# Split attention heads: the product with v in two passes, the sums of rows on VectorE

## The chip, the cores and the metric

The kernel runs on one core of a Trainium2 chip. The metric is the device time of one execution in microseconds. Three executions of the kernel before took 1229.11, 1231.16 and 1234.45 us; the median is 1231.16 us.

The engines are called as in the profile: PE is TensorE's matmul and PEld its loads of weights, DVE is VectorE, ACT is ScalarE, POOL is GpSimd, SP is the queue that issues most DMAs.

## The reference

Attention with a decay that is summed along the sequence, over 64 heads (8 batches of 8 heads, 576 positions, 64 columns a head), and then an MLP with a squared ReLU over all 4608 tokens:

```
scores = q @ k.T / 8
cum = cumsum(log(clip(f, 1e-4, 1)))
scores = where(causal, -1e9, scores + cum[i] - cum[j])
attn = exp(scores - max(scores)); attn /= sum(attn) + 1e-9
x = heads of attn @ v side by side          # 4608 x 512
out = relu(x @ w_in)**2 @ w_out             # 512 -> 2048 -> 512
```

Everything is float32.

## The kernel before, in words

**Two kinds of heads.** TensorE takes float32 whole, which is slow, or in the rounded type fp32r, which is fast. The first 14 heads (`NWHOLE`) work on whole numbers. The other 50 are *split*: a number is a rounded high part and a rounded rest, and a product of two numbers is made of passes over the parts. The MLP is split throughout (x into xh and xl, the weights and g likewise). This text is about the split heads.

**Units and slots.** A head has six units, in this order (keys in blocks of 128, the last of 64):

| unit | key block | queries | columns |
|---|---|---|---|
| 0 | 0 | 256 to 575 | 320 |
| 1 | 2 | 256 to 575 | 320 |
| 2 | 3 | 384 to 575 | 192 |
| 3 | 4 | 512 to 575 | 64 |
| 4 | 1 | 128 to 575 | 448 |
| 5 | 0 | 0 to 255 | 256 |

Scores stand transposed: keys on the partitions, queries along the columns. One slot (the loop over `n`, lines 684 to 710) traces one unit's scores and whatever is due beside them. In the slot of a unit stand, in this order: its scores and exp (`score`, lines 356 to 391), the products with v of the unit two slots earlier (`LAG` is 2; `av_part`, lines 413 to 448), a step of a finished pair of heads (`finish`), events of the first half, `fill(n, 0.5)`, events of the second half, `fill(n, 1.0)`. Each of PE, ACT, DVE, POOL and (after the opening) SP keeps the order of tracing.

**A split unit.** Two matmuls make the scores (lines 371 and 374). ACT takes exp into p (line 384); where the block lies on the diagonal (units 1 to 5), POOL masks its first square (line 386). `split_p` (lines 393 to 403) then makes ph, rounded by ACT (line 399), and the rest pl on DVE (line 400). It is put off: `split_last` traces it when the next MLP half is placed, or at the latest at the next slot's start. `av_split` (lines 405 to 411) makes three passes into the bank: high part of v with pl, rest of v with ph, high part of v with ph. The high part of v has a 65th column of ones, so that row 64 of the bank is the sum of p over the keys, the softmax's denominator.

**The bank of the products.** While the MLP runs there is one bank, 0. The queries 256 to 575 (the right part) gather in it over units 0 to 4; ACT then copies the result (line 446) and the row of denominators (line 448) out. Queries 0 to 255 (the left part) follow in the same bank, from unit 5 and a piece of unit 4, in unit 1's slot of the next head, and are copied out likewise.

**A pair of heads** is divided together (lines 450 to 474), in four parts at slots that `DIVIDE` gives, counted from the slot after the pair's last unit, less one: the denominators go to a compact tile by DMA (part 0), DVE adds 1e-9 and takes reciprocals and a DMA stores them to memory (part 1), two DMAs spread each row over 64 partitions of `den` (part 2), and POOL multiplies (part 3, line 473). `den` has two buffers, `wmag` (the weights' magnitudes, line 181) has one.

**v.** `load_v` fetches v of a head; `split_v` (lines 305 to 314) rounds it on DVE (line 311) and takes the rest on POOL (line 312), in the second half of unit 4's slot of the head before.

**q and k** are loaded into `qkraw` and rounded by `prep` (lines 285 to 303): r2 and kl0 on DVE, l2 and r1 on ACT, the rests on POOL.

**The MLP** is placed between the units in halves: `mlp1` (lines 497 to 515: twelve matmuls of 256 columns into bank 4, then r on ACT, g = r * r on DVE, gh = r * r rounded on ACT, gl = g - gh on DVE), and `mlp2` (lines 517 to 533: six matmuls of 512 columns) of the step before. `fill` (lines 604 to 622) counts how many halves are to be done at n + part: they are spread evenly from `ready[b-1]` to `ready[b]`, where `ready` is the slot of part 3 of the batch's last pair plus 2 (line 602). A batch lets 2, sometimes 3, chunks of 256 tokens run, of 32 halves each; the 48 slots of a batch thus hold 64 halves, once 96. `split_x` (lines 479 to 495) rounds x for a chunk on DVE.

## Time and profile before

| | |
|---|---|
| median of three executions | 1231.16 us |
| the profiled execution's own time | 1234.24 us |
| its span, first to last instruction | 1232.5 us |
| mean granted clock of TensorE | 0.990 |
| PE busy | 1181.0 us (96%) |
| PEld busy | 1048.0 us (85%) |
| DVE busy | 775.6 us (63%) |
| ACT busy | 700.0 us (57%) |
| POOL busy | 409.0 us (33%) |

Matmuls are pipelined: a matmul's busy time overlaps the next one's, so what one costs is read from the distance between starts or from the chain of waits, not from its mean duration. On DVE and ACT, too, the next instruction may start a little before the last has ended. In the views a row is a start, a duration, the engine, the line, the operation, out<-in and the shape; in square brackets stands the idle time of the engine before it and what ended it.

The first 14 heads and the conversion of the weights take about the first 200 us; the split heads follow to about 1080 us; the rest is MLP alone.

### The profile page before, as it was taken

What the parts mean: (1) busy time and instruction counts of PE and PEld (TensorE: products, weight loads), DVE (VectorE), ACT (ScalarE), POOL (GpSimd) and SP (SyncE); (2) the same over time, 40 slices, a digit from 0 to 9 for tenths busy, and PEclk for the clock granted to TensorE, in tenths of its full rate; (3) what the DMA queues carried; (4) which work ended last, traced back from release to release, by engine and by line L of the source; (5) the groups of instructions that cost most, each with busy time, mean ns of one, the idle gap of its engine ahead of it and who ended that gap; (6) DMA issues with size and microseconds to landing.
All of it is one profiled execution on the core that took longest, in us unless ns stands there. A gap on an engine that the chain in (4) does not pass through costs nothing.

```text
span 1232.5 us, 23332 instructions
## 1 busy us (share of the span) xinstructions
PE 1181.0 (96%) x7652; PEld 1048.0 (85%) x7652; DVE 775.6 (63%) x2045; ACT 700.0 (57%) x1720; POOL 409.0 (33%) x669
## 2 busy tenths in 40 slices
PE   4886999999999999999999999999999999999998
PEld 2554887888998899999999989998998899999997
DVE  7667875677676767666655676667676667533322
ACT  2563655566666566665655666666666666633232
POOL 4563544433333333332222233334333433200000
PEclk9997999999999999999999999999999999999999
DMA  7887531111121212121102121212121212000000
GB/s 178 184 169 173 160 102 43 36 49 41 42 58 41 59 37 49 33 56 36 49 16 58 27 58 42 58 36 49 32 58 42 58 41 58 12 27 1 18 18 18
DMA packets 114978, 71.62 MB, mean 58 GB/s; under 512 B 96909, under 2 KB 96909, under 8 KB 114857
## 3 DMA queue, kind: packets, MB, share of 16 engines
q1 hardware_dynamic: 113736, 66.00, 22.0%
q0 software_dynamic: 1120, 4.13, 1.8%
q8 instruction: 61, 1.00, 0.3%
q14 instruction: 61, 0.49, 0.1%
HBM read 59.90 MB, written 9.87 MB: 57 GB/s over the span
## 4 chain that ended last, share of the span: by engine, by line
PE 85%; DMA 5%; DVE 3%; ACT 3%; issue 2%; POOL 1%; SPq 1%; DVEq 0%; POOLq 0%; ACTq 0%
PE bank L503 32%; PE bank L526 30%; PE bank L326 3%; PE bank L409 3%; PE bank L374 3%; PE bank L411 3%; PE bank L410 3%; PE bank L371 3%; DMA rl<-tcol 2%; PE bank L432 2%; PE bank L365 2%; DVE bank L332 1%; DMA w<-in_w_in 1%; ACT den L448 0%; ACT r L511 0%
## 5 line engine op out<-in xcount | busy, mean ns | idle before, releaser
L526 PE MATMUL bank<-w,gh 128*128 128x512 f32 x1152 | 414.1, 400 | 0.0
L503 PE MATMUL bank<-xh,w 128*128 128x256 f32 x2304 | 331.9, 287 | 2.8 <-DVE tcol L332 2.2
L503 PEld LDWEIGHTS bank<-xh,w 128*128 128x128 f32 x2304 | 302.8, 190 | 11.4 <-DVE tcol L332 2.4
L400 DVE TENSOR_TENSOR pl<-p,ph 128x320 fp32r<-128x320 f32 (+4 forms) x300 | 182.1, 607 | 202.7 <-ACT ph L399 196.1
L526 PEld LDWEIGHTS bank<-w,gh 128*128 128x128 f32 x1152 | 217.5, 189 | 38.4
L526 PE MATMUL bank<-w,gl 128*128 128x512 f32 x576 | 226.8, 394 | 0.1
L511 ACT ACTIVATE r<-bank 128x256 f32<-128x256 f32 x288 | 110.3, 383 | 199.2 <-PE bank L503 181.0
L512 DVE TENSOR_TENSOR g<-r 128x256 f32<-128x256 f32 x288 | 128.6, 447 | 145.2 <-ACT r L511 144.6
L386 POOL TENSOR_SCALAR_AFFINE_SELECT p<-p 128x128 f32<-128x128 f32 (+1 forms) x250 | 80.8, 323 | 417.3 <-ACT p L384 276.1
L399 ACT CAST ph<-p 128x320 fp32r<-128x320 f32 (+4 forms) x300 | 124.4, 415 | 151.1 <-POOL p L386 149.3
L503 PE MATMUL bank<-xl,w 128*128 128x256 f32 x1152 | 185.0, 283 | 0.0
L503 PEld LDWEIGHTS bank<-xl,w 128*128 128x128 f32 x1152 | 159.0, 191 | 0.0
L384 ACT ACTIVATE p<-bank 128x320 f32<-128x320 f32 (+4 forms) x300 | 115.9, 386 | 64.9 <-PE bank L374 53.4
L514 DVE TENSOR_TENSOR gl<-g,gh 128x256 fp32r<-128x256 f32 x288 | 127.2, 442 | 35.0 <-PE bank L526 0.5
L332 DVE CUSTOM_DVE_ANT_0 bank<-bank,mz 128x256 f32<-128x256 f32 (+4 forms) x320 | 133.1, 432 | 24.7 <-PE bank L326 20.6
L326 PE MATMUL bank<-rk 66*128 66x320 f32 (+9 forms) x384 | 109.2, 315 | 22.9 <-DMA rk<-qkraw 10.6
L513 ACT ACTIVATE gh<-r 128x256 fp32r<-128x256 f32 x288 | 120.4, 418 | 9.2
L526 PEld LDWEIGHTS bank<-w,gl 128*128 128x128 f32 x576 | 109.2, 190 | 14.1 <-DVE gl L514 0.9
L409 PE MATMUL bank<-pl,vh 128*65 128x320 f32 (+4 forms) x350 | 96.8, 277 | 2.3 <-ACT den L448 2.3
L214 POOL TENSOR_TENSOR w<-osb,w 128x128 fp32r<-128x128 f32 x128 | 72.9, 597 | 77.9 <-ACT w L210 57.5
L326 PEld LDWEIGHTS bank<-rk 66*128 66x128 f32 (+3 forms) x384 | 68.3, 185 | 32.4 <-DVE tcol L332 12.6
L410 PE MATMUL bank<-ph,v 128*64 128x320 f32 (+4 forms) x350 | 94.6, 270 | 0.0
(83 smaller groups left out, 1558.3 us busy)
## 6 DMA issues: line engine op xcount, KB each, us to landing
qkraw<-in_qk SPq DMA_DIRECT2D x50, 288.0 KB
v<-in_v SPq DMA_DIRECT2D x62, 160.0 KB
out<-osb SPq DMA_DIRECT2D x36, 256.0 KB
den<-rdr SPq DMA_DIRECT2D x62, 144.0 KB
w<-in_w_in SPq DMA_DIRECT2D x16, 512.0 KB
w<-in_w_out SPq DMA_DIRECT2D x16, 512.0 KB
rk<-in_qk POOLq DMA_DIRECT2D x14, 288.0 KB, 5.4
rl<-in_qk SPq DMA_DIRECT2D x14, 288.0 KB
```

The source lines that it names most:

```text
L326: nc.tensor.matmul(ps[:m, :n], st["r2"][:rows, q0:q0 + m], st["kl0"][:rows, k0:k0 + n], start=True, stop=True,)
L332: nc.vector.tensor_tensor_reduce(out=ps[:m, :n], in0=ps[:m, :n], in1=mz[:m, mo:mo + n], op0=ALU.add, op1=ALU.min, scale=-1.0, scalar=init, ...
L384: nc.scalar.activation(out=p[:kn, :n], in_=ps[:kn, :n], func=AF.Exp, scale=SCALE)
L399: nc.scalar.copy(out=ph[:, :n], in_=p[:, :n])
L400: nc.vector.tensor_tensor(out=pl[:, :n], in0=p[:, :n], in1=ph[:, :n].bitcast(F32), op=ALU.subtract,)
L409: nc.tensor.matmul(acc[:D + 1, o], vh, pl[:, i], start=first, stop=False)
L410: nc.tensor.matmul(acc[:D, o], vl, ph[:, i], start=False, stop=False)
L503: nc.tensor.matmul(ph[:, :T], w[:, s, cc], x[:, cc, :], start=(cc == 0 and k == 0), stop=(cc == NCC - 1 and k == 2),)
L512: nc.vector.tensor_tensor(out=g, in0=r, in1=r, op=ALU.mult)
L513: nc.scalar.activation(out=gh, in_=r, func=AF.Square)
L514: nc.vector.tensor_tensor(out=gl, in0=g, in1=gh.bitcast(F32), op=ALU.subtract)
L526: nc.tensor.matmul(po, g[:, ts], w[:, s], start=(fc == 0 and k == 0), stop=(fc == NF - 1 and k == 2),)
```

## The change

**Products with v.** The tile of a head's v now holds the high part in columns 0 to 63 and the rest in 64 to 127. One pass of all 128 columns with ph gives the high product in the bank's rows 0 to 63 and the rest's product in rows 64 to 127; a second pass of 64 columns adds the high part with pl. The first product of a bank starts with the wide pass, so that it clears all 128 rows. Instead of the row of denominators, ACT copies rows 64 to 127 out, to a tile xl; when the pair is divided, DVE adds xl to x.

**Sums of rows.** As there is no column of ones, the denominators come from p itself, by `sum_p` right behind `split_p`. Units 0 and 5 write exp straight into a tile `total` (128 x 576, in the buffer of `wmag`), DVE adds the other units' p to it, and reduces it over 32 keys at a time with a transposing reduction: after unit 4 for the right part (320 columns), after unit 5 for the left (256). A DMA (`store_sums`) writes four partial sums for each query to memory; `finish` fetches those of a pair, adds them with 1e-9 in a fifth place, takes reciprocals and stores them in two DMAs.

**Buffers and order.** `den` has one buffer in turn, which xl and the spread denominators share. `DIVIDE` for batches after the first is 2, 4, 5, 6 and no longer 2, 4, 6, 7. As `ready` follows from its last entry, the split of a batch's first x and the start of its MLP move one slot earlier too. v of the first eight heads lies in buffers of weights that are converted later, and v of heads 8 to 13 is fetched three slots later. `qkraw` is one fixed tile; whole heads put their row of denominators in its row 64.

**MLP and q.** g is squared on ACT, from r, and no longer multiplied on DVE. The rest of q is taken against r2 (DVE's rounding) and no longer against r1 (ACT's).

```diff
     def split_v(h):
         if NWHOLE <= h < NH:
             st = state[h]
             vr = st["vr"][:, :, :D]
-            vh = st["vh"] = vhs[h % 2]
-            st["vl"] = wk.tile([P, NJ, D], F32R, name="v", bufs=3)
-            nc.vector.tensor_copy(out=vh[:, :, :D], in_=vr)
+            v = st["vhl"] = vhls[h % 2]
+            nc.vector.tensor_copy(out=v[:, :, :D], in_=vr)
             nc.gpsimd.tensor_tensor(
-                out=st["vl"], in0=vr, in1=vh[:, :, :D].bitcast(F32), op=ALU.subtract,
+                out=v[:, :, D:], in0=vr, in1=v[:, :, :D].bitcast(F32), op=ALU.subtract,
             )
...
         st["p"][u] = ph, pl
+        sum_p(h, u, p)
+
+    def sum_p(h, u, p):
+        st = state[h]
+        _, q0, q1 = UNITS[u]
+        total = totals[0]
+        def add(p, q0, q1):
+            nc.vector.tensor_tensor(
+                out=total[:, q0:q1], in0=total[:, q0:q1], in1=p, op=ALU.add,
+            )
+        def columns(o, q0, q1):
+            n = (q1 - q0) // 32
+            nc.vector.tensor_reduce(
+                out=st["sums"][:, o:o + n], in_=total[:, q0:q1].rearrange("p (i c) -> p c i", c=n),
+                axis=mybir.AxisListType.X, op=ALU.add, apply_transpose=True,
+            )
+        if 0 < u < NU - 1:
+            add(p[:, max(QA - q0, 0):q1 - q0], max(q0, QA), q1)
+            if q0 < QA:
+                st["rest"] = p[:, :QA - q0], q0, QA
+        if u == NU - 2:
+            st["sums"] = wk.tile([P, NC], F32, name="sums")
+            columns(0, QA, S)
+        if u == NU - 1:
+            add(*st.pop("rest"))
+            columns(NH1, 0, QA)
+
+    def store_sums(h):
+        st, i = state[h], h % 2
+        st["sdr"] = state[h - 1]["sdr"] if i else dr.tile([4, D, NC], F32, name="sdr")
+        nc.sync.dma_start(out=st["sdr"][:, i * 32:(i + 1) * 32], in_=st["sums"])
 
     def av_split(st, acc, u, o, i, first, last):
         j = UNITS[u][0]
         ph, pl = st["p"][u]
-        vh, vl = st["vh"][:, j, :D + 1], st["vl"][:, j, :]
-        nc.tensor.matmul(acc[:D + 1, o], vh, pl[:, i], start=first, stop=False)
-        nc.tensor.matmul(acc[:D, o], vl, ph[:, i], start=False, stop=False)
-        nc.tensor.matmul(acc[:D + 1, o], vh, ph[:, i], start=False, stop=last)
+        vhl = st["vhl"][:, j]
+        high = acc[:, o], vhl, ph[:, i]
+        low = acc[:D, o], vhl[:, :D], pl[:, i]
+        for k, args in enumerate((high, low) if first else (low, high)):
+            nc.tensor.matmul(*args, start=first and k == 0, stop=last and k == 1)
...
             nc.scalar.copy(out=x, in_=acc[:D, :n])
-            m = D if replicated(h) else 1
-            nc.scalar.copy(out=st["den"][o:o + m, base:base + n], in_=acc[D:D + m, :n])
+            if h >= NWHOLE:
+                nc.scalar.copy(out=st["xl"][o:o + D, base:base + n], in_=acc[D:, :n])
...
+            else:
+                nc.vector.tensor_tensor(out=x, in0=x, in1=st["xl"], op=ALU.add)
+                r = wk.tile([P, NC], F32, name="sums")[:D]
+                nc.vector.tensor_reduce(
+                    out=r, in_=parts.rearrange("p g c -> p c g"), axis=mybir.AxisListType.X, op=ALU.add,
+                )
+                nc.vector.reciprocal(out=r, in_=r)
+                for o, q0, q1 in (0, QA, S), (NH1, 0, QA):
+                    nc.sync.dma_start(
+                        out=st["rdr"][:, q0:q1].rearrange("h (p c) -> h p c", p=32),
+                        in_=r[:, o:o + (q1 - q0) // 32],
+                    )
         if part == 2:
+            den = st["den"] = wk.tile([P, S], F32, name="den", bufs=1)
...
-        nc.vector.tensor_tensor(out=g, in0=r, in1=r, op=ALU.mult)
+        nc.scalar.activation(out=g, in_=r, func=AF.Square)
         nc.scalar.activation(out=gh, in_=r, func=AF.Square)
...
-    DIVIDE = (2, 6, 9, 13), (2, 4, 6, 7)
+    DIVIDE = (2, 6, 9, 13), (2, 4, 5, 6)
...
+            at((h + 1) * NU, 1, store_sums, h)
```

88 lines of the change are left out of this document (54 added, 34 removed).

## The prediction

> **What bounds the kernel now.** I read the page first, then the busy times by stretches, the chain of waits through two heads, and the order of time of the same stretch on all engines.
>
> The page: span, busy time of TensorE, and the granted clock in 40 slices.
>
> ```profile
> span 1232.5 us, 23332 instructions
> PE 1181.0 (96%) x7652; PEld 1048.0 (85%) x7652; DVE 775.6 (63%) x2045; ACT 700.0 (57%) x1720; POOL 409.0 (33%) x669
> PEclk9997999999999999999999999999999999999999
> ```
>
> Busy time by stretches (span, then PE, PEld, DVE, ACT, POOL): one among the split heads.
>
> ```profile
> 300.00:350.00 50.00, 50.00 (x344) 45.69 (x343) 34.95 (x95) 33.28 (x84) 17.28 (x28) 1.00 0.19 46
> ```
>
> TensorE is never idle in it, at clock 1.00. DVE and ACT are two thirds busy among the heads. Time taken off TensorE is therefore gained, if the engines that empty the banks can follow. The chain of waits through the same heads (start, us on the chain) prices each piece of TensorE's work:
>
> ```profile
> 859.77 0.21 PE bank L371
> ...
> 860.27 0.09 PE bank L410
> ...
> 862.21 0.06 PE bank L410
> ...
> 862.33 1.51 PE bank L503 x12
> 863.84 1.39 PE bank L526 x6
> 865.24 0.15 PE bank L371
> ...
> 865.68 0.15 PE bank L410
> ...
> 865.98 1.43 PE bank L503 x12
> ...
> 867.83 0.12 PE bank L410
> ...
> 868.13 0.06 PE bank L410
> ...
> 870.00 0.28 PE bank L409
> ```
>
> A pass costs 0.21, 0.15, 0.12, 0.09, 0.06 and 0.06 us at 448, 320, 256, 192, 128 and 64 columns, an mlp1 1.43, an mlp2 1.39. The last row is a wait of 0.13 (0.28 against 0.15): unit 0's product finds bank 0 not yet emptied.
>
> **What TensorE saves.** Line 410 goes: per split head three passes of 320 columns, one each of 256, 192, 128, 64: 0.45 + 0.12 + 0.09 + 0.06 + 0.06 = 0.78 us. The kept high pass now has 128 weight columns, not 65. Twelve mlp1 matmuls behind a 64-column pass take 1.51, behind a 320-column pass 1.43: a load of 128 weight columns needs 0.08 more than the 0.03 that 64 columns move (half of the 0.06 at 128), so 0.11. Against passes of 0.12 and more it is hidden. At 192 columns it gives back 0.03, at 128 and 64 nearly all. I take 0.45 + 0.12 + 0.06 + 0.01 = 0.64 us a head, 32 us for 50 heads (bounds: 0.78 and 0.57, the long passes alone, 39 and 28). The Trainium skill (TensorE: Matmul & The Clock Gate, LDWEIGHTS) says that a load takes its columns over 1.2 ns, 107 ns for 128 and 54 for 65; the trace agrees. By that page the three loads of a product (65 + 64 + 65 columns) and the two left (64 + 128) take the same time.
>
> **What moves besides.** DIVIDE for the later batches loses a slot at its end, and `ready` hangs on it. From the second boundary on, `fill` places the MLP one slot earlier against the units. Working `goal` out at 64 halves in 48 slots: before, mlp1 falls at unit 0, mlp2 at 1, both at 2, mlp1 at 3, mlp2 at 4, both at 5. After: mlp2 at 0, both at 1, mlp1 at 2, mlp2 at 3, both at 4, mlp1 at 5. This helps the wait in the 870.00 row (now an mlp1 more lies ahead of it); I give 4 us of the 5 that 0.13 makes in 40 heads. But it puts an mlp1 ahead of `split_v`, and the order of time shows what hangs on that. One head from unit 4's scores to the left part's product:
>
> ```profile
> 859.81 0.37 PE L374 MATMUL bank<-rl 128*128 128x448 f32 x1
> 859.85 0.38 ACT L511 ACTIVATE r<-bank 128x256 f32<-128x256 f32 x1 [1.42 <-PE bank L503]
> 860.02 0.25 PE L409 MATMUL bank<-pl,vh 128*65 128x192 f32 x1
> 860.27 0.42 ACT L513 ACTIVATE gh<-r 128x256 fp32r<-128x256 f32 x1
> 860.59 0.53 ACT L384 ACTIVATE p<-bank 128x448 f32<-128x448 f32 x1
> 860.80 0.42 DVE L514 TENSOR_TENSOR gl<-g,gh 128x256 fp32r<-128x256 f32 x1
> 862.17 0.63 DVE L400 TENSOR_TENSOR pl<-p,ph 128x448 fp32r<-128x448 f32 x1 [0.75 <-ACT ph L399]
> 862.71 0.35 DVE L311 CAST vh<-v 128x320 fp32r<-128x320 f32 x1
> 863.20 0.88 POOL L312 TENSOR_TENSOR v<-v,vh 128x320 fp32r<-128x320 f32 x1 [1.67 <-PE bank L409]
> 864.03 0.29 POOL L386 TENSOR_SCALAR_AFFINE_SELECT p<-p 128x128 f32<-128x128 f32 x1
> 864.35 0.41 ACT L399 CAST ph<-p 128x256 fp32r<-128x256 f32 x1 [1.75 <-POOL p L386]
> 864.67 0.38 ACT L511 ACTIVATE r<-bank 128x256 f32<-128x256 f32 x1
> 865.08 0.42 ACT L513 ACTIVATE gh<-r 128x256 fp32r<-128x256 f32 x1
> 865.57 0.44 ACT L384 ACTIVATE p<-bank 128x320 f32<-128x320 f32 x1
> 866.02 0.42 ACT L446 COPY xt<-bank 64x320 f32<-64x320 f32 x1
> 866.46 0.42 ACT L448 COPY den<-bank 1x320 f32<-1x320 f32 x1
> 867.55 0.28 PE L409 MATMUL bank<-pl,vh 128*65 128x256 f32 x1
> ```
>
> Read it as one chain in strict queues: DVE's cast of v (L311), POOL's rest of v (L312), POOL's mask of unit 5 behind it, ACT's ph, then r and gh, then the next exp, then the two copies that free bank 0. It ends at 866.88; TensorE needs the bank at 867.55. That is 0.67 us to spare, and ACT stands idle 1.75 us in the middle because L312 is ahead of the mask.
>
> **The same chain after the change**, counted from 860.02. TensorE: product of unit 2 0.20, maximum 0.03, mlp1 1.43, mlp2 1.39, scores 0.24, unit 3's product 0.14, mlp1 1.51, scores 0.30, product of unit 4 0.30, mlp2 1.39, scores 0.30: it wants bank 0 at 7.23. ACT and DVE: mlp1 ends at 1.66; r 0.25 later (the L511 row at 859.85; its mlp1 ended a pass of 0.21 ahead of the L374 row, at 859.60) at 1.91; g now on ACT 0.41 later (864.67 to 865.08) at 2.32; gh 0.32 later (860.27 to 860.59) at 2.64; gl 0.53 behind it at 3.17; L311 only now, as `fill` puts that mlp1 ahead of `split_v`, at 3.51 (before: 2.69). Then as in the rows: L312 +0.49, mask +0.83, ph +0.32, r +0.32, g +0.41, gh +0.32, exp +0.32, copies +0.45 and +0.44, end +0.42: 7.83. TensorE waits about 0.6 us in each such head.
>
> The sums: per head five additions and two reductions on DVE, less four g (L512), plus one addition of 576 and two small ones a pair.
>
> ```profile
> L512 DVE TENSOR_TENSOR g<-r 128x256 f32<-128x256 f32 x288 | 128.6, 447 | 145.2 <-ACT r L511 144.6
> L332 DVE CUSTOM_DVE_ANT_0 bank<-bank,mz 128x320 f32<-128x320 f32 x64 | 32.3, 505 | 5.9 <-PE bank L326 4.7
> L491 DVE TENSOR_TENSOR xl<-xt,xh 128x512 fp32r<-128x512 f32 x4 | 2.8, 692 | 0.1
> ```
>
> Unit 4's addition and reduction of 320 stand between pl and L311: 0.5 each by the L332 row. They run from 2.2 to 3.2, just before gl could start, so they hide, as long as the reduction costs under 0.6. The trace has no transposing reduction; its bounds are 0.35 (L311's 320 columns) and 1.0 (twice the L332 row). At 1.0 the chain ends 0.4 later. I take 0.5, the nearest reducing row.
>
> **The one buffer of `den`.** The new copy of the right part's low half (xl) shares it with the broadcast denominators, so in every second head ACT's second copy waits until POOL has multiplied the pair before:
>
> ```profile
> 858.81 0.53 SPq L467 DMA_DIRECT2D rdr<-cmp  x1
> ...
> 861.57 0.55 SPq L470 DMA_DIRECT2D den<-rdr  x1
> ...
> 862.81 0.59 SPq L470 DMA_DIRECT2D den<-rdr  x1
> ...
> 866.00 1.43 POOL L473 TENSOR_TENSOR xt<-xt,den 128x576 f32<-128x576 f32 x1 [1.68 <-DMA den<-rdr]
> ```
>
> From the second broadcast to the product: 3.19 us, plus 1.43. After: DVE reaches part 1 behind gl of unit 2's mlp1: that mlp1 ends 2.42 ahead of the count's start (scores 0.42, maximum 0.09, mlp2 1.39, maximum 0.15, product 0.29, scores 0.08), r, g, gh, gl and the next start add 0.25, 0.41, 0.32, 0.53 and 0.34, so -0.6; addition 0.7 (L491 at 512), two small ones 0.4, stores at 0.6 and 1.2, landed between 1.8 (an issue's length) and 4.0 (858.81 to 861.57 is an upper bound of 2.76). Broadcasts a slot earlier than now, at the landing and 0.6 to 1.24 later; product ends between 7.0 and 9.9, so the copy ends 7.4 to 10.3 against 7.23 wanted. The lower end is no worse than the ACT chain; I take 1.4 us for these heads, between 0.6 and the 2.2 of a landing in 2.0.
>
> Other DMAs: SP issues the sums (one a head), one fetch for two and two stores for one a pair, at 0.53 to 0.59 each (rows above); the second store is counted, the rest fill a queue that is empty most of the time. Behind the broadcasts, which wait for the stores' landing, stand the maxima of the queries 0 to 63, which only unit 5's scores read, two slots on. The moved loads of v, the fixed `qkraw` and q's rest against r2 lie in slots with nothing due behind them: 0, and at most a product's 0.15 a head if not.
>
> **Sum.** 40 heads (20 pairs) lie in batches with 64 halves; the batch with 96 has two halves in each slot, spare time, and keeps its gain. -32 - 4 + 20 x (0.6 + 1.4) = +4. Once in a batch DVE's split of x now stands before the product rather than behind; the waits view has it so far as
>
> ```profile
> DVE xh L490 <- POOL xt L473: 10.6, 6, 2.4
> ```
>
> and a slot of 2.7 earlier makes up to 1 us on TensorE in five batches: +4. So +8: 1242 in the profiled execution's terms (1234.24, itself 3.1 over the median of 1231.16), **1239** by the median. This case alone spans 1213 (stalls 0.3 and 0.7) to 1262 (0.9 and 2.2).
>
> **Rivals.** (1) TensorE stays the bound and all of this hides: -36, 1195. For it: DVE and ACT are a third idle; against it: the spare 0.67 is one place, not a share. It decides for it if the copies end 0.6 earlier than I count. (2) Only the `den` buffer bites, 0.9 a pair: -18, 1213. (3) The weight loads bind, not the columns: 0.06 x 3 before, 0.06 + 0.11 after, per product, so nothing is saved: 1231. The 0.15 at 320 columns against a load of 0.11 speaks against it. The Trainium skill (Perfetto Trace Analysis, Identifying the Most-Contended Engine) would judge TensorE by its loads' busy share, here 85%. (4) DVE becomes the bound with reductions over 1 us: another 1 us in 40 heads, 1279.
>
> **Chances.** Forecast 0.54 (faster 0.06, same 0.13, slower 0.35); (1) 0.25, faster; (2) 0.08 (0.06 faster, 0.02 same); (3) 0.04 (0.03 same, 0.01 slower); (4) 0.09, slower. Under 0.5% a measurement of this kernel cannot tell from no change. Faster 0.37, same 0.18, slower 0.45. The range 1195 to 1262 leaves out half of (1) and most of (4); the forecast's own is 1213 to 1262.
>
> **What would show it.** Right: no third pass, and a new wait of the left part's product (unit 5) on ACT's second copy, 0.6 in odd heads and longer in even ones, there behind POOL's product; L311 behind gl; PE busy under 96%. Wrong: that wait absent, and TensorE as full as now.

## The result, and the profile after

The changed kernel takes **1342.25 us** (median of four executions, 1339.91 to 1345.48), the kernel before 1231.47 us beside it: a ratio of 1.090 (95% interval 1.0865 to 1.0935), 111 us slower. The forecast was 1239 us, slower by 8, with a range that ended at 1262. The sign of the likeliest case was right; the size was off by more than ten times. One of the four executions of two_sp_v below took 3739 us and is left out, so that its time is the median of three.

The page of the changed kernel (own time of the profiled execution 1340.81 us, mean granted clock 0.964 where it was 0.990):

```profile
span 1338.8 us, 22723 instructions
PE 1197.0 (89%) x7302; PEld 1053.6 (79%) x7302; DVE 798.7 (60%) x2132; ACT 780.3 (58%) x2008; POOL 411.7 (31%) x668
```

There are 350 matmuls fewer, as the change says: seven passes in each of 50 heads. Yet PE's busy time has grown from 1181.0 to 1197.0 us, and its share has fallen from 96% to 89%. DVE and ACT are below two thirds: no engine has taken TensorE's place as the bound. Busy times in two stretches (span, then PE, PEld, DVE, ACT, POOL with their instructions, granted clock, share and rate of DMA), one among the heads with 64 halves a batch and one that holds most of the batch with 96:

```profile
300.00:400.00 100.00, 87.59 (x540) 78.94 (x540) 63.26 (x174) 59.81 (x157) 32.41 (x50) 0.95 0.18 41
...
600.00:700.00 100.00, 98.95 (x652) 90.19 (x652) 64.99 (x173) 64.61 (x168) 28.61 (x45) 1.00 0.17 43
```

Before, the first of these was at 99% and clock 1.00. TensorE now stands idle 12 us in 100, and what it does it does at a lower clock; in the batch that has MLP work to spare, both are as before. The waits, longest in total first (us in all, times, longest):

```profile
POOL xt L551 <- DMA den<-rdr: 99.2, 31, 17.3
PE bank L464 <- ACT den L504: 70.8, 41, 3.9
ACT den L504 <- POOL xt L551: 54.5, 24, 3.7
DVE xh L568 <- POOL xt L551: 40.1, 7, 6.7
PE bank L381 <- DMA rk<-tcol: 12.3, 25, 0.9
```

The second row is the wait that the prediction named as its sign: the product with v (L464) on ACT's second copy (L504). Worked out from the starts of the matmuls, the left part's product is late by 3.12 us on average in 20 even heads and by 0.71 us in 21 odd ones. Measured by the distance between the masks of unit 3 of consecutive heads (outside the batch with 96 halves), the step to the next head was 16.24 and 16.50 us before, in turn, and is 16.72 and 21.09 us now. Every second head pays most of it.

One even head in order of time (start, us, engine, line, operation; in brackets the idle time before it and what ended it), from DVE's part 1 to the copy, rows of other work left out:

```profile
850.71 0.79 DVE L535 TENSOR_TENSOR xt<-xt,den 128x576 f32<-128x576 f32 x1
850.96 1.82 POOL L314 TENSOR_TENSOR rl<-qkraw,rk 64x576 fp32r<-64x576 f32 x1
851.76 0.26 DVE L540 RECIPROCAL sums<-sums 64x18 f32<-64x18 f32 x1
852.80 0.52 SPq L250 DMA_DIRECT2D qkraw<-in_qk  x1
853.42 1.14 SPq L542 DMA_DIRECT2D rdr<-sums  x2
854.66 1.79 SPq L347 DMA_DIRECT2D rk<-tcol  x3
854.84 0.78 DVE L434 TRANSPOSE_TENSOR_REDUCE sums<-wmag 128x10 f32<-128x320 f32 x1
855.53 0.40 DVE L592 TENSOR_TENSOR gl<-g,gh 128x256 fp32r<-128x256 f32 x1
855.83 0.37 DVE L321 CAST vhl<-v 128x320 fp32r<-128x320 f32 x1
856.34 0.81 POOL L322 TENSOR_TENSOR vhl<-v,vhl 128x320 fp32r<-128x320 f32 x1 [3.19 <-issue]
856.67 1.13 SPq L549 DMA_DIRECT2D den<-rdr  x2
857.11 0.29 POOL L401 TENSOR_SCALAR_AFFINE_SELECT wmag<-wmag 128x128 f32<-128x128 f32 x1
859.10 0.41 ACT L502 COPY xt<-bank 64x320 f32<-64x320 f32 x1
860.39 1.40 POOL L551 TENSOR_TENSOR xt<-xt,den 128x576 f32<-128x576 f32 x1 [2.99 <-DMA den<-rdr]
861.82 0.42 ACT L504 COPY den<-bank 64x320 f32<-64x320 f32 x1 [2.31 <-POOL xt L551]
```

Three things stand in it. The copy L504 waits for POOL's product, as predicted. The product waits for broadcasts (L549) that were issued 4.6 us after the reciprocals (L540) had ended at 852.02; the stores (L542) went out only at 853.42, behind a load of q and k (L250) that waited for POOL's rest of q (L314, until 852.78), and three issues of maxima (L347, until 856.45) stand between the stores and the broadcasts. In 23 of the 25 pairs the first store goes out 1.40 us or more after the reciprocals' end. And beside it the other chain runs, with L321 behind gl and L322 ahead of the mask, as predicted.

TensorE in the next even head:

```profile
894.64 0.31 PE L384 MATMUL bank<-rl 128*128 128x320 f32 x1
898.12 0.47 PE L464 MATMUL bank<-ph,vhl 128*128 128x256 f32 x1 [3.17 <-ACT den L504]
899.59 0.58 PE L464 MATMUL bank<-pl,vhl 128*64 128x256 f32 x2 [1.00 <-DVE pl L415]
...
900.19 2.02 PE L581 MATMUL bank<-xh,w 128*128 128x256 f32 x8
```

After the wait the eight matmuls of mlp1 take 2.02 us, where they took 1.19 at 855.00 in the same trace: half the clock. From 215 us to the end, matmuls that follow each other at 1.6 to 2.4 times their usual distance cost 44 us in this trace and 9 us in that of before, where the granted clock is 1.00 from 215 to 1230 us, so that a few us of each are the method's own error. Of 21 waits of TensorE of 2.8 us or more, 20 are followed, within some 5 us of their beginning, by such a stretch of 2.8 to 6 us, mostly 3.4.

### The profile page after: what moved, and what is told of

Read it like the earlier page. It is cut to its first block, busy times and chain, and to the rows that moved or that the text cites. A ratio compares the mean times of both kernels' runs of the same rounds, so it can differ in the third digit from the quotient of the medians.

```text
span 1338.8 us, 22723 instructions
## 1 busy us (share of the span) xinstructions
PE 1197.0 (89%) x7302; PEld 1053.6 (79%) x7302; DVE 798.7 (60%) x2132; ACT 780.3 (58%) x2008; POOL 411.7 (31%) x668
## 3 DMA queue, kind: packets, MB, share of 16 engines
q1 hardware_dynamic: 122836, 66.80, 20.8%
## 5 line engine op out<-in xcount | busy, mean ns | idle before, releaser
L581 PE MATMUL bank<-xh,w 128*128 128x256 f32 x2304 | 346.8, 294 | 8.8 <-DVE xh L568 4.1
L401 POOL TENSOR_SCALAR_AFFINE_SELECT p<-p 128x128 f32<-128x128 f32 x200 | 65.5, 327 | 415.5 <-ACT p L399 307.3
L415 DVE TENSOR_TENSOR pl<-p,ph 128x320 fp32r<-128x320 f32 x200 | 133.8, 669 | 75.9 <-ACT ph L414 75.5
L464 PE MATMUL bank<-ph,vhl 128*128 128x320 f32 (+4 forms) x350 | 109.2, 312 | 71.2 <-ACT den L504 70.8
L342 DVE CUSTOM_DVE_ANT_0 bank<-bank,mz 128x256 f32<-128x256 f32 (+4 forms) x320 | 133.9, 433 | 22.3 <-PE bank L336 17.8
L464 PEld LDWEIGHTS bank<-ph,vhl 128*128 128x128 f32 x350 | 67.8, 194 | 86.4 <-ACT den L504 82.3
L415 DVE TENSOR_TENSOR pl<-wmag,ph 128x320 fp32r<-128x320 f32 x100 | 45.9, 459 | 146.3 <-ACT ph L414 146.3
L414 ACT CAST ph<-p 128x320 fp32r<-128x320 f32 x200 | 81.2, 406 | 87.8 <-POOL p L401 87.2
L590 ACT ACTIVATE g<-r 128x256 f32<-128x256 f32 x288 | 120.5, 418 | 11.6 <-DVE gl L592 2.5
L381 PE MATMUL bank<-rk 67*128 67x320 f32 (+4 forms) x300 | 90.0, 300 | 13.6 <-DMA rk<-tcol 12.3
L399 ACT ACTIVATE p<-bank 128x320 f32<-128x320 f32 x200 | 75.5, 378 | 37.5 <-PE bank L384 36.2
```

The lines of the kernel that those rows point to most:

```text
L342: nc.vector.tensor_tensor_reduce(out=ps[:m, :n], in0=ps[:m, :n], in1=mz[:m, mo:mo + n], op0=ALU.add, op1=ALU.min, scale=-1.0, scalar=init, ...
L381: nc.tensor.matmul(ps[:kn, :n], st["kl0"][:D + 3, k0:k0 + kn], st["r2"][:D + 3, q0:q1], start=True, stop=False,)
L414: nc.scalar.copy(out=ph[:, :n], in_=p[:, :n])
L415: nc.vector.tensor_tensor(out=pl[:, :n], in0=p[:, :n], in1=ph[:, :n].bitcast(F32), op=ALU.subtract,)
L464: nc.tensor.matmul(*args, start=first and k == 0, stop=last and k == 1)
L581: nc.tensor.matmul(ph[:, :T], w[:, s, cc], x[:, cc, :], start=(cc == 0 and k == 0), stop=(cc == NCC - 1 and k == 2),)
```

## The experiments

All runs, with the ratio to the kernel before on the same chip. "Two buffers" is for den; "SP traced" is SP's queue in the order of tracing throughout.

| run | edit | median us | ratio, 95% interval |
|---|---|---|---|
| the changed kernel | | 1342.25 | 1.090 (1.0865, 1.0935) |
| two_den | two buffers | 1313.73 | 1.068 (1.065, 1.071) |
| sp_traced | SP traced | 1296.71 | 1.053 (1.049, 1.056) |
| busy_wait | matmuls in the idle time | 1324.18 | 1.077 (1.073, 1.081) |
| before_two | before, third pass out | 1205.56 | 0.980 (0.977, 0.983) |
| two_sp | two buffers, SP traced | 1307.41 | 1.061 (1.057, 1.065) |
| two_sp_slots | and DIVIDE as before | 1313.10 | 1.067 (1.064, 1.071) |
| no_xl_all | DVE adds out of the bank, SP traced, DIVIDE as before, g on DVE | 1361.53 | 1.106 (1.102, 1.109) |
| before_slots | before, DIVIDE of the change | 1236.03 | 1.0054 (1.0034, 1.0075) |
| two_sp_v | two_sp, split of v later | 1274.80 | 1.036 (1.033, 1.040) |
| sp_v | sp_traced, split of v later | 1276.90 | 1.037 (1.034, 1.040) |
| two_sp_vq | two_sp_v, rest of q and split of x later | 1253.19 | 1.020 (1.016, 1.024) |
| two_sp_nosum | two_sp, no sums | 1271.28 | 1.033 (1.030, 1.035) |
| fit_a | two_sp_vq, copies ahead of exp | 1242.52 | 1.010 (1.008, 1.012) |
| fit_b | the like, one buffer, g on DVE | 1288.33 | 1.049 (1.045, 1.052) |
| fit_c | fit_a, broadcasts behind the load | 1269.55 | 1.033 (1.030, 1.035) |
| fit_d | fit_c, MLP a slot later | 1282.66 | 1.044 (1.042, 1.046) |
| fit_e | fit_c, product a slot later | 1255.85 | 1.022 (1.020, 1.024) |
| fit_a1 | fit_a, one buffer | 1266.75 | 1.033 (1.029, 1.036) |

### What TensorE's saving is worth

```diff
-        nc.tensor.matmul(acc[:D + 1, o], vh, pl[:, i], start=first, stop=False)
-        nc.tensor.matmul(acc[:D, o], vl, ph[:, i], start=False, stop=False)
-        nc.tensor.matmul(acc[:D + 1, o], vh, ph[:, i], start=False, stop=last)
+        vh = st["wide"][:, j * (D + 2):min(j * (D + 2) + P, VW + 30)]
+        high = acc[:vh.shape[1], o], vh, ph[:, i]
+        low = acc[:D + 1, o], vh[:, :D + 1], pl[:, i]
+        for k, args in enumerate((high, low) if first else (low, high)):
+            nc.tensor.matmul(*args, start=first and k == 0, stop=last and k == 1)
```

> The kernel before with its third pass (rest of v with ph) left out, and 128 (for the block of 64 keys 96) weight columns in the pass of high v with ph; the first product of a bank begins with that pass. The rest of v is still computed; its product with ph is left out, nothing else. Theory A (TensorE is the bound, a pass costs its columns): 28 to 39 us less than 1231, at 32: 1199. Theory B (the loads of weights bind): 1228 to 1234. Theory C (the banks' path binds as soon as TensorE is faster): 5 to 20 us less, with a wait of the left part's product on ACT's copies of 0.3 to 0.6 us a head.

Measured: 24 us less than before, between A and C. Theory B (loads of weights bind) falls: half the passes' loads now have 128 columns, and the time fell. In the trace the left part's product now waits for ACT's second copy in 21 heads:

```profile
PE bank L415 <- ACT den L452: 6.6, 21, 0.5
```

So already the old order has a chain that ends close behind TensorE. Where nothing waits, the saving is what the prediction worked out: in the batch with 96 halves a head takes 21.19 us here and 21.77 before, 0.58 less, and 0.63 less in fit_a below, where the rest of the change is in (forecast: 0.64).

### One buffer, or the queue that feeds it

```diff
-                    st["xl"] = state[h - 1]["xl"] if h % 2 else wk.tile([P, S], F32, name="den", bufs=1)
+                    st["xl"] = state[h - 1]["xl"] if h % 2 else wk.tile([P, S], F32, name="den")
...
-            den = st["den"] = wk.tile([P, S], F32, name="den", bufs=1)
+            den = st["den"] = wk.tile([P, S], F32, name="den")
...
-                vr = wk.tile([P, NJ, D + 2], F32, name="v")
+                vr = wk.tile([P, NJ, D], F32, name="v", bufs=1)
...
-        g = wk.tile([P, T], F32, name="g", bufs=1)
+        g = r
...
+        nc.scalar.activation(out=gh, in_=r, func=AF.Square)
         nc.scalar.activation(out=g, in_=r, func=AF.Square)
-        nc.scalar.activation(out=gh, in_=r, func=AF.Square)
```

> The changed kernel (1342) with two buffers for den in turn, so that the copy of xl waits for the addition of the pair before and no longer for POOL's product. Room for it: v of a split head in one buffer, g written over r (gh first), the identity for the masks in a tile of its own, v of heads 8 to 13 in the buffers of p. Theory A, the one buffer costs nearly all: the wait of the left part's product on ACT's second copy of every second head (about 3 us in 20 heads) goes, and with it the stretches of lower clock behind it (mean granted clock 0.964, back to 0.99): 1240 to 1260. Theory B, the added us are spread over the earlier MLP slots, the longer ACT chain and the loads: the wait moves elsewhere and no more than 30 us come back: 1310 or more.

```diff
-    in_order(tc, [mybir.EngineType.SP], opening)
+    in_order(tc, [mybir.EngineType.SP])
```

> The changed kernel with SP's queue held to the order of tracing throughout, not only through the opening. In the changed kernel's trace the load of q and k, which waits for POOL's rest of q, is issued 0.6 us ahead of the two stores of the reciprocals although it is traced a slot later. Theory A (the stores and so the broadcasts are late by that load): stores 0.7 to 1.3 us earlier in 20 heads, the stall 1 us shorter, and some of the lower clock gone: 1290 to 1325. Theory B (the landing of the stores and of the broadcasts sets the stall, or other DMAs now come late): 1335 to 1355.

The second buffer gives 28 us, far from the 82 to 102 of its theory A and within its theory B, by which the wait moves elsewhere; the queue's order gives 45, within its theory A. With two buffers ACT no longer waits for POOL's product, but the left part's product is late in *every* head, by 0.93 us on average: the chain past L321 and L322 (here L324 and L325), which had been hidden in the even heads behind the longer wait. It ends so:

```profile
857.17 0.78 DVE L437 TRANSPOSE_TENSOR_REDUCE sums<-wmag 128x10 f32<-128x320 f32 x1
857.87 0.38 DVE L595 TENSOR_TENSOR gl<-r,gh 128x256 fp32r<-128x256 f32 x1
858.17 0.48 DVE L324 CAST vhl<-v 128x320 fp32r<-128x320 f32 x1
858.78 0.86 POOL L325 TENSOR_TENSOR vhl<-v,vhl 128x320 fp32r<-128x320 f32 x1 [3.31 <-issue]
859.60 0.29 POOL L404 TENSOR_SCALAR_AFFINE_SELECT wmag<-wmag 128x128 f32<-128x128 f32 x1
859.93 0.41 ACT L417 CAST ph<-wmag 128x256 fp32r<-128x256 f32 x1 [1.92 <-POOL wmag L404]
...
862.29 0.42 ACT L507 COPY den<-bank 64x320 f32<-64x320 f32 x1
...
862.76 0.39 PE L467 MATMUL bank<-ph,vhl 128*128 128x256 f32 x1 [0.89 <-ACT den L507]
```

In sp_traced the buffer is as in the change, and ACT's waits for POOL's product still shrink, by the waits of ACT from 230 to 1100 us, from 50.0 us (longest 3.7) to

```profile
ACT den L504 <- POOL xt L551: 12.5, 19, 1.8
```

The product itself comes earlier: the first store now goes out 0.03 us after the reciprocals in each of the 25 pairs (median of the change: 1.41), and the first broadcast 2.00 us after the second store (2.85), both by the median. The wait was thus less the buffer's than that of the chain of DMAs which gives the buffer back. sp_traced orders all of SP's issues anew, though, so that its 45 us are the price of the queue's order as a whole and not of that one load.

### The clock

```diff
+    def fill_wait(h):
+        st = state[h]
+        ps = bank("s")
+        for _ in range(10):
+            nc.tensor.matmul(ps[:, :448], st["vhl"][:, 0], st["p"][4][0], start=True, stop=True)
...
+                if ha >= NWHOLE and ha % 2 == 0:
+                    fill_wait(ha)
                 av_part(ha, ua, True)
```

> The changed kernel with ten matmuls of 448 columns (0.206 us each, 2.06 in all), whose result nobody reads, ahead of the left part's product in every even split head, where TensorE stands idle for about 3 us. Theory A (the idle time itself lowers the clock for some us after it): idle time of about 1 us, granted clock back to 0.98 or more, and 20 to 35 us less than the changed kernel although TensorE gets 41 to 50 us of work more: 1305 to 1322. Theory B (the lower clock has another cause, or costs nothing): the matmuls only fill idle time, 1338 to 1346. Theory C (the wait begins later when the matmuls are there, the buffer is given back by PE's own pace): 40 us more, 1380.

```profile
894.29 2.20 PE L470 MATMUL bank<-ph,vhl 128*128 128x448 f32 x10
897.22 0.38 PE L464 MATMUL bank<-ph,vhl 128*128 128x256 f32 x1 [0.73 <-ACT den L510]
```

25 heads times 2.06 us are 51 us of useless work, and the kernel is 18 us *faster*, at a mean granted clock of 0.983 instead of 0.964 (0.991 to 0.993 in its other three executions); matmuls at half speed cost 21 us instead of 44. Theories B and C fall. The time ends 2 us above the range of A: in the batch with 96 halves there was no idle time to fill, and four heads there take 1.7 to 3.3 us longer. A wait of 3 us thus costs about another 1.7 us (35 us over 20 heads) in the clock behind it.

Shorter waits can do it too. In fit_b below the left part's product waits about 2 us in every second head; of 17 such waits of 1.9 to 2.1 us, 10 are followed by a stretch at a granted clock of 0.50. Of the waits of 2.8 us or more above, nearly all were. Here the granted clock is 0.50 from 900.1 to 903.4 us:

```profile
900.38 0.58 PE L469 MATMUL bank<-ph,vhl 128*128 128x256 f32 x1 [1.99 <-ACT den L509]
...
901.29 2.02 PE L586 MATMUL bank<-xh,w 128*128 128x256 f32 x8
```

### No single cause: the edits together

two_sp has the edits of two_den and of sp_traced.

> Both edits at once: two buffers for den in turn (alone 1314) and SP's queue in the order of tracing (alone 1297). Theory A (two ways to be late with the same thing, the second buffer leaves the queue nothing to spoil): about as the better of the two, 1285 to 1300. Theory B (they remove different waits, the copy of xl on the one side, late maxima in r2 and late fetches on the other): most of both gains, 1342 - 28 - 45 = 1269, within 10.

> The same, and DIVIDE for the later batches as in the kernel before (2, 4, 6, 7), so that the MLP halves and the split of a batch's first x stand a slot later again. Theory A (the earlier slot puts DVE's cast of v behind gl, and DVE's split of x ahead of POOL's product of the pair): the wait of about 1 us in every head and that of about 4 us at each of five batch boundaries go, 1269 - 40 - 20 = 1210, at least 35 us less than two_sp. Theory B (the length of ACT's work, g with it, sets the wait in every head, wherever the halves stand): only the boundaries gain, 15 to 25 us less than two_sp.

In two_sp_slots `DIVIDE = (2, 6, 9, 13), (2, 4, 6, 7)` stands again. Both runs miss both theories. Two edits together (1307) are worse than one of them (1297): the wait on ACT's copies is 57.6 us, the queue has nothing left to spoil in the even heads, and all heads are on the chain. Another 16.1 us go to matmuls of the maxima that wait for a DMA (10.0 in sp_traced). Which of the edits that made room for the buffer lengthens the odd heads (17.32 us against 16.79 in sp_traced) wasn't tried. With the old slots the boundaries do gain, but mlp1 then waits for ACT's r and a product for POOL's mask, in each head:

```profile
PE bank L584 <- ACT r L592: 46.1, 40, 2.0
PE bank L467 <- POOL p L404: 35.8, 37, 1.1
```

So the old slots seem to fit the old lengths of work on ACT and DVE, not the new ones; no run changes these lengths alone.

```diff
-            nc.scalar.copy(out=x, in_=acc[:D, :n])
+            nc.scalar.copy(out=x, in_=acc[D if h >= NWHOLE else 0:, :n][:D])
             if h >= NWHOLE:
-                nc.scalar.copy(out=st["xl"][o:o + D, base:base + n], in_=acc[D:, :n])
+                nc.vector.tensor_tensor(out=x, in0=x, in1=acc[:D, :n], op=ALU.add)
```

> xl without a buffer: ACT copies the bank's rows 64 to 127 (product of the rest) to x, and DVE adds the bank's rows 0 to 63 to it, so the addition at part 1 falls away; with SP in the order of tracing, DIVIDE as before, and g on DVE again. den has one buffer. Theory A: nothing waits for POOL's product any more, and DVE has the time: 1195 to 1215, faster than the kernel before. Theory B (DVE, behind additions and reductions, comes late to the bank): a wait of the left part's product on DVE of 0.5 to 1 us in each of 50 heads, 1225 to 1250.

It is theory B in kind, but 111 us above the range of B: the bank now waits for DVE, twice in a head. The run also has SP in the order of tracing, the old DIVIDE and g on DVE, so that its time doesn't price DVE's addition alone.

```profile
PE bank L464 <- DVE xt L502: 96.4, 80, 2.3
```

> The kernel before with DIVIDE (2, 4, 5, 6) for the later batches, and nothing else of the change: the MLP halves and the split of x one slot earlier. Theory A (the earlier slot puts the cast of v behind gl and lengthens the way to the copies; the split of x comes before the product): 8 to 40 us more than 1230, with a new wait of the left part's product on ACT in most heads and of the products on DVE at the boundaries. Theory B (the slot matters only with the sums on DVE and g on ACT): 1225 to 1234, the wait of 0.13 on bank 0 gone.

The slots alone, in the kernel before, cost 7 us (1.0054, interval 1.0034 to 1.0075), between its two theories. The chain of theory A is not there: ACT's copy holds the left part's product 0.4 us in all. What is there is the boundary, where products wait for DVE, which, as I read it, stands at the split of x:

```profile
PE bank L409 <- DVE pl L400: 7.8, 5, 2.3
```

Inside the batches with 64 halves every second head gains instead, 16.35 to 16.03 us on average. The two traces differ by only 0.4 us in span (1232.9 and 1232.5), so that they do not show where the 7 us between the medians lie.

### The chain, link by link

```diff
-    VLOAD, VSPLIT = (-1, 2), 4
+    VLOAD, VSPLIT = (-1, 2), 5
```

> two_sp (1307: two buffers for den, SP in the order of tracing) with the split of v one slot later (VSPLIT 5), so that DVE's cast of v and POOL's rest of v stand behind unit 5's mask and no longer ahead of it. Theory A (a chain over all engines sets the pace of the heads: addition, reduction, gl, cast of v, rest of v, mask, ph, r, gh, g, exp, copies): the mask of unit 5 comes about 1.5 us earlier, the wait of 0.9 to 1.7 us on ACT's copies in each of 40 heads goes: 1255 to 1275. Theory B (the work merely moves to another place of the chain): 1295 or more.

> sp_traced (1297: one buffer for den, SP in the order of tracing) with the split of v one slot later (VSPLIT 5). Theory A (the one buffer and the chain both hold the copies, whichever ends last): the odd heads gain about 1 us, the even ones next to nothing, as they still wait for POOL's product: 1275 to 1290, slower than two_sp_v. Theory B (with the chain shortened the product comes early enough): equal to two_sp_v within 5 us.

This one number is worth 33 us (two_sp_v, within its theory A) and 20 us (sp_v): the cast of v and its rest stood in a chain that set the pace. The odd heads fall from 17.32 to 16.08 and from 16.79 to 15.99 us. The two times lie 2 us apart, less than the executions of either scatter, so at this point the second buffer is worth next to nothing; that is theory B of sp_v.

```diff
-    SPLIT = 0, 1, 1, 3
+    SPLIT = 0, 1, 1, 4
...
-            at((h - 2) * NU + LOAD, 0, load, h)
...
-                at((h - 1) * NU + SPLIT[part], 1, prep, h, part)
+                at((h - 1) * NU + SPLIT[part], int(part < 3), prep, h, part)
+            at((h - 2) * NU + LOAD, 1, load, h)
...
-        at(ready[b] - 1 - (b > 0), 0, split_x, b * S // T, b + 1)
+        at(ready[b] - 1, 0, split_x, b * S // T, b + 1)
```

> two_sp_v with POOL's rest of q (576 columns, 1.5 us) behind unit 4's mask instead of ahead of it, the load of the next q and k behind it, and DVE's split of a batch's first x one slot later. Theory A (the same chain further up, and the split of x waiting at the head of DVE's queue at five boundaries): 15 to 35 us less than two_sp_v. Theory B (the chain no longer binds, or q and k come late now): within 8 us of two_sp_v, or slower with a wait of the scores on rl.

22 us less, in the range of theory A, but hardly from the rest of q: the heads inside a batch stay as they were (16.1 and 16.5 to 17.1 us). The six heads at the boundaries gain: from 20.9 to 24.0 us down to 17.8 to 20.8, 22 us in all. DVE had stood before the split of x until POOL had multiplied the batch's last pair, with everything traced behind it. Both edits are in the one run, so that it is the place of the gain that points to the split of x.

```diff
         st["p"][u] = ph, pl
-        sum_p(h, u, p)
```

> two_sp (1307) without the sums on DVE: no additions and no transposing reductions, the denominators are left out (ones are stored in their place, by the same DMAs). Theory A (addition 0.48 and reduction 0.78 of unit 4 stand ahead of gl and of the cast of v, in the chain that sets the pace): 0.9 to 1.3 us less in 40 to 50 heads, 1250 to 1270. Theory B (they hide, as DVE would wait for ACT's g otherwise): 1295 or more.

36 us less than two_sp, theory A but for 1 us: the sums did not hide. (The run leaves the denominators out; ones are stored in their place.) The odd heads fall by 0.74 us, the others by 1.37. What they cost on DVE (columns: count, busy us, mean ns), in the changed kernel:

```profile
L428 DVE TENSOR_TENSOR wmag<-wmag,p 128x320 f32<-128x320 f32 x100 | 50.7, 507 | 0.0
L434 DVE TRANSPOSE_TENSOR_REDUCE sums<-wmag 128x10 f32<-128x320 f32 x50 | 38.5, 771 | 1.7
```

### Whether a version beats both

fit_a traces ACT's two copies of the right part ahead of unit 0's exp, and the first step of q's and k's rounding half a slot earlier:

```diff
-            score(h, u)
+            late = score(h, u)
...
                 av_part(ha, ua, False)
...
+        if live and late:
+            late()
```

> two_sp_vq (1253) with ACT's two copies of the right part ahead of the next head's first exp instead of behind it, and the first step of q and k's rounding half a slot earlier. Theory A (the copies still end the chain that TensorE waits for, 0.3 to 0.5 us in 40 heads, and DVE's rounding of k holds the maxima by 0.7 to 1.3 us in every second head): both waits go, 20 to 35 us less: 1218 to 1233. Theory B (the exp that now comes 0.85 us later is missed at once): 1250 or more, with a wait on ph or pl of unit 0.

fit_b has the same edits on the kernel with one buffer and `nc.vector.tensor_tensor(out=g, in0=r, in1=r, op=ALU.mult)` in place of ACT's square; fit_a1 is fit_a with `bufs=1` at both tiles of den.

> The same edits on the kernel with one buffer for den (sp_traced with the split of v, the rest of q, the split of x, the copies and the rounding of q and k moved), and g squared on DVE as in the kernel before. Theory A (ACT's squaring stands in the chain, DVE has room, and the one buffer no longer ends last): equal to fit_a or up to 10 us less. Theory B (the one buffer still holds the copies in every second head): 10 to 25 us more than fit_a, the wait of the left part's product on ACT's copies in the even heads alone.

> fit_a (1242.5) with one buffer for den, nothing else. Theory A (the one buffer holds ACT's second copy until POOL has multiplied the pair before; nothing else is late there any more): a wait of 2 to 3.4 us of the left part's product on ACT's second copy in 20 heads, and some lower clock behind it: 1275 to 1295. Theory B (what fit_b lost came from the squaring on DVE): within 8 us of 1242.

fit_a lies between its two theories. The wait on the copies is gone, and the odd heads take 15.54 us, 0.70 less than before the change: TensorE's saving, in full. It is missed by every second head and by the boundaries (waits of TensorE, fit_a):

```profile
PE bank L589 <- DVE xh L576: 17.6, 6, 4.1
...
PE bank L339 <- DVE rk L307: 10.7, 14, 1.4
```

The rounding of k is late because SP holds the load of q and k behind the broadcasts, which wait for the stores' landing. fit_a1 is theory A in kind, not in size: one buffer costs 24 us where its theory had 32 to 52, and in fit_a1

```profile
PE bank L472 <- ACT den L512: 37.0, 24, 2.9
```

So a second buffer is worth 28 us (two_den), nothing or less (two_sp, two_sp_v) or 24 us, by what else is late. fit_b takes 22 us more than fit_a1 and 46 more than fit_a, beyond both its theories. It has g on DVE, but also the two buffers of v and the order of g and gh of the change, so that what of it is the squaring is not settled.

Three tries at what is left in fit_a, none of which helped:

```diff
         for args in fins.get(n, ()):
-            finish(*args)
+            if args[1] != 2 or args[0] < NWHOLE:
+                finish(*args)
...
         for do in events.get((n, 1), ()):
             do()
+        for args in fins.get(n, ()):
+            if args[1] == 2 and args[0] >= NWHOLE:
+                finish(*args)
```

> fit_a (1242.5) with the two broadcasts of a pair issued behind the load of the next q and k instead of ahead of it; both are traced in the same slot, and SP waits at the broadcasts for the reciprocals' landing. Theory A (in every second head the load, held behind the waiting broadcasts, brings q and k 1 us late, DVE rounds k late, and the maxima hold TensorE by 0.9 us): that wait goes, 15 to 22 us less: 1220 to 1228, faster than the kernel before. Theory B (the broadcasts come late in turn, the product of the pair holds the split of x): within 5 us of 1242.

```diff
-    ready = [fin(b * H + H - 1, 3) + 2 for b in range(B)]
+    ready = [fin(b * H + H - 1, 3) + 2 + (b > 0) for b in range(B)]
...
-        at(ready[b] - 1, 0, split_x, b * S // T, b + 1)
+        at(ready[b] - 1 - (b > 0), 0, split_x, b * S // T, b + 1)
```

> fit_c with the MLP of each later batch begun one slot later (as in the kernel before), the split of its first x where it was. Theory A (at five boundaries mlp1 waits 2 to 4 us for the split of x, which waits for the last pair's product): 8 to 15 us less than fit_c. Theory B (the halves stand worse against the units, as two_sp_slots showed with a wait of mlp1 on ACT's r and of products on POOL's mask): 10 to 40 us more than fit_c.

```diff
-    DIVIDE = (2, 6, 9, 13), (2, 4, 5, 6)
+    DIVIDE = (2, 6, 9, 13), (2, 4, 5, 7)
...
-    ready = [fin(b * H + H - 1, 3) + 2 for b in range(B)]
+    ready = [fin(b * H + H - 1, 3) + 2 - (b > 0) for b in range(B)]
```

> fit_c (1270) with POOL's product of a pair one slot later (DIVIDE 2, 4, 5, 7), behind POOL's rest of v, and the beginning of the MLP and the split of x in the slots they had. Theory A (in fit_c the product, waiting for its broadcasts at the head of POOL's queue, holds the rest of v and so the next head's first products; with q and k early and the rest of v ahead of the product neither wait is left): 1220 to 1235. Theory B (the product now holds POOL's rest of q or a mask, there is no place in POOL's queue where it waits for nothing): 1245 or more, with a wait of a product on POOL in the even heads.

fit_c is 27 us slower than fit_a, outside both its theories. The wait on the rounding of k is gone, and others have come for it (waits of TensorE from 210 us on): the broadcasts and so the product are later, POOL's rest of v stands behind the product, and the boundaries wait longer.

```profile
PE bank L589 <- DVE xh L576: 22.1, 6, 4.0
PE bank L472 <- POOL vhl L325: 7.3, 14, 0.8
```

fit_d loses 13 us more by the halves' new places, its theory B; fit_e takes the wait on POOL's rest of v away, but is 13 us above fit_a, in the range of its theory B, though with 20.1 us of waits for the split of x in place of the wait on POOL that B expected. None of these versions beats the kernel before. fit_a comes nearest, 1.0% slower. Whether an order exists in which every head takes fit_a's 15.5 us stays open.

## Why the prediction was wrong

**The step that failed** is "The one buffer of `den`": "I take 1.4 us for these heads, between 0.6 and the 2.2 of a landing in 2.0". Measured were 3.12 us in 20 heads. By its own terms, counted as there from unit 2's product (851.47 in the even head above):

| term | prediction | measured |
|---|---|---|
| DVE reaches part 1 | -0.6 | -0.8 (850.71) |
| stores issued | 0.6 and 1.2 | 1.95 (853.42) and 2.6 |
| first broadcast | 1.8 to 4.0 | 5.2 (856.67) |
| second broadcast to product | 3.19 | 3.2 |
| product ends | 7.0 to 9.9 | 10.3 (861.79) |
| copy ends | 7.4 to 10.3, taken 8.6 | 10.8 |
| TensorE wants the bank | 7.23 | 7.8 |

The engines' terms hold within 0.6 us. What fails is SP's queue, twice: 1.35 us at the stores, and then 2.6 us from the second store to the first broadcast, of which three issues of maxima (L347, 854.66 to 856.45) fill 1.8. The landing itself cannot be read there. In sp_traced, with two such issues between, the same distance is 2.00 us; the 2.76 that the prediction took for its upper bound, from the kernel before, had a load and two maxima in it. The prediction said that other DMAs "fill a queue that is empty most of the time" and placed among the maxima only those that come behind the broadcasts. But a load that waits for POOL held the stores behind it (852.80 and 853.42), and three issues of other maxima stood ahead of the broadcasts. The text ahead of the prediction says that SP too keeps the order of tracing after the opening; that is wrong. The call with `opening` as its end chains SP's instructions only up to there, and the trace shows a load, traced a slot later than the stores, issued ahead of them. sp_traced puts a price on the order of the whole queue: 45 us.

**What was not in the sum at all** is the clock. The prediction read "clock 1.00" off the stretches and worked out waits, but not what a wait does to the matmuls behind it: 35 us here, and busy_wait shows that it is the idle time that does it. The Trainium skill (TensorE: Matmul & The Clock Gate, Why this matters for your kernels) warns of idle gaps of TensorE above about 3 us, after which it runs at half rate; the trace agrees, with half speed for mostly 3.4 us after 20 of 21 waits of 2.8 us or more, where a wait costs half as much again. But the bound is not as sharp as that: half speed followed 10 of fit_b's 17 waits of 1.9 to 2.1 us, and one of 1.75 us in the changed kernel (before 1163.05). By the 3 us the prediction's upper bound of 2.2 us a head would have been free of it; by these rows some of the price would have come even there.

**The sum, with measured sizes:** 77 us of waits on the copies (20 times 3.12 and 21 times 0.71), 35 of lower clock, 12 of maxima that come late by DMA, some 5 of left products waiting for pl at the boundaries, less the 32 saved: 97 of the 106 us between the two spans. The rest is not assigned. Against the forecast the waits on the copies are 37 us more (77, where 20 heads of 1.4 and 20 of 0.6 make 40), the clock 35 and the maxima 12, which the sum had at nothing.

**The other steps.** The saving of 0.64 us a head is right: 0.58 to 0.70 wherever nothing waits. The chain through the cast of v behind gl, 0.6 us in each odd head, is right in place and near in size (0.71); two_sp_v shows that it is this chain, since moving the split of v alone gives 33 us. Its reduction took 0.77 us, not 0.5, inside the bounds of 0.35 and 1.0, and "hide, as long as the reduction costs under 0.6" thereby fails as stated: two_sp_nosum has 36 us for the sums. That POOL's rest of q holds unit 4's mask (L314 until 852.78, the mask after it) was not counted. The boundaries were put at 4 us; the row quoted for them grew from 10.6 to 40.1 us, and the run with the later split of x (two_sp_vq) gained 22 us there. The slots' gain of 4 us from the 870.00 row did not come as a net gain: before_slots is 7 us slower, although every second head inside its batches is 0.3 us shorter. The lower end of the forecast's own range, 1213, does not follow from its terms: stalls of 0.3 and 0.7 in 20 heads each, less 36, make 1215, and 1219 with the 4 us of the boundaries; nothing hangs on it.

**The rivals.** (2), only the `den` buffer bites, has the right mechanism for most of the loss (the even heads), but its price of 0.9 us a pair was far too small, and two_den shows that removing it alone uncovers the next chain. (1), TensorE stays the bound, falls with PE at 89%. (3), the loads bind, falls with before_two. (4), DVE as the bound, falls with DVE at 60%: DVE was late in its order, never full.

## What to carry to other kernels

When work moves off the bound engine into a tightly ordered schedule, price the chain round all engines for one period, queues of DMAs included: an engine that is a third idle can still be late in every period, and several chains that end within a microsecond of each other hide one another, so that mending one uncovers the next and prices do not add. Find out who really orders each queue, and read in the trace what stands ahead of an issue, not how full the queue is. Where TensorE waits 3 us in a period, add half as much again for the clock, and expect some of that from about 2 us on; try filling the wait before trusting a sum of waits.

## What was not expected of the hardware

That ten useless matmuls ahead of a wait make a kernel 18 us faster, by the clock: see busy_wait.

And that DVE's instructions wait out POOL's subtractions. In fit_a, the same subtraction twice, once alone and once begun while POOL takes the rest of q:

```profile
870.98 0.47 DVE L423 TENSOR_TENSOR pl<-wmag,ph 128x320 fp32r<-128x320 f32 x1
...
871.58 1.43 POOL L314 TENSOR_TENSOR rl<-qkraw,rk 64x576 fp32r<-64x576 f32 x1
...
872.13 1.22 DVE L423 TENSOR_TENSOR pl<-p,ph 128x320 fp32r<-128x320 f32 x1 [0.69 <-ACT ph L422]
```

The second takes 1.22 us and ends 0.34 after POOL's, as if most of its work came when that was done. The like holds in the kernel before (median 0.86 us where it begins beside a POOL subtraction, 0.49 alone): 43 of 46 such instructions end 0.35 us after POOL's, whether they take 0.69 or 1.23. So it is in both sums; but durations taken from one row carry it unseen to another place. The Trainium skill (SBUF — State Buffer, Terms) says that the two share a pair of ports, which one holds for a whole instruction while the other waits; these rows agree.
